# The last supertile of a 1x1 depthwise-separable convolution, worked off tile by tile

## The chip, the core and the metric

The kernel runs on one core of one Trainium2 chip. A core has a matrix engine (TensorE, PE in the profile, with its weight loads listed as PEld), a vector engine (VectorE, DVE), a scalar engine (ScalarE, ACT), GpSimd (POOL), and SyncE (SP), which here issues the transfers; sixteen DMA engines move data between the device memory and the on-chip buffer. TensorE writes its sums to a separate accumulator memory (the `ps` tiles)[...]. The metric is the device time of one execution in microseconds (us), lower is better; the profile's span is a little shorter than that time because it runs from the first to the last instruction.

## What is computed

```python
x:  (1, 384, 384, 384) bf16     # batch, height, width, channels
dw: (1, 1, 384) bf16            # depthwise weights, one tap (k = 1)
pw: (384, 384) bf16             # pointwise weights

out = x * dw[0, 0]              # k = 1: no neighbours, no padding
return einsum("bhwc,cd->bhwd", out, pw)
```

With one tap the depthwise part is a scaling of the channels, so the whole is one matrix product: 147,456 rows of 384 channels times a 384 x 384 matrix whose row c is `dw[c] * pw[c]`. Each of x and the output is 113 MB.

## The kernel before

The 147,456 rows are worked off in 288 *supertiles* of 512 rows. A supertile passes four stations: its x lies in the on-chip buffer with rows on the partitions; DVE transposes it in 32 x 32 blocks of 32-bit words (two channels in a word), so that channels lie on the partitions; TensorE multiplies; ACT copies the four accumulators to an output buffer as bf16; SyncE stores. Transfers are grouped by ten supertiles (`LMAX`), in three rotating x buffers and three rotating output buffers; the first and the last groups are cut smaller.

```python
def _groups(n_super):
    head, tail = [[1, 1, 2, 2, 4]], [[6, 4], [4, 2, 1, 1]]   # the last two supertiles are chunks of their own
    ...
LONG, LONG_AT = 2, [8, 148]     # the last two supertiles' x is loaded at supertiles 8 and 148
```

The block transposes leave each 32-row group of partitions with another set of x rows. Group q of partitions holds a 32-word slice of channels of the rows of accumulator q, so one supertile is four independent products of 32 partitions each, run at the same time on four row groups of the array. The weights `w_r` are laid out so that every group of 32 partitions holds the same channel pairs:

```python
steps = [(b, par) for b in range(4) for par in range(2)] + [(4, 0), (5, 0), (4, 1), (5, 1)]

def supertile(s, rv):
    for b, par in steps:                     # 6 channel blocks x 2 channels of a word: 12 groups
        for q in range(4):                   # 4 matmuls of 32 rows, at the same time
            if q == 0 and par == 0 and b in (0, 3):
                nc.tensor.wait_ge(s_t[s][b // 3], rv)
            ...
            mm = nc.tensor.matmul(
                PS[s][:, q, :D],
                lhsT=Ts[s][32 * q : 32 * q + 32, b, par::2],
                rhs=w_r[32 * q : 32 * q + 32, b, par, :],
                start=(b, par) == steps[0], stop=(b, par) == steps[-1],
                tile_position=(32 * q, 0))
            if (b, par) == steps[0] and q == 0:
                mm._wait_ge(s_a[s], rv)      # the accumulators were copied out
            if (b, par) in ((2, 1), (5, 1)) and q == 3:
                mm.then_inc(s_pe)            # half done, all done
...
with nc.tensor.Fori(0, NS // 2, 1) as it:    # all 288 supertiles, two per turn of the loop
    rv = nc.tensor.to_reg(it + 1)
    for s in range(2):
        supertile(s, rv)
```

All four accumulators of a supertile end in its last group. The copies out, by ACT alone except for the very last supertile:

```python
for jj, (t, j) in enumerate(order):
    s = jj % 2
    ...
    if jj + 1 == NS:                         # last supertile: two copies on ACT, two on DVE
        nc.vector.wait_ge(s_pe, 2 * jj + 2)
        ...
        nc.scalar.wait_ge(s_pe, 2 * jj + 2)
        for q in (0, 2):
            nc.scalar.copy(Ov[:, q, j, :], PS[s][:, q, :D]).then_inc(s_a[s])
            nc.vector.tensor_copy(Ov[:, q + 1, j, :], PS[s][:, q + 1, :D]).then_inc(s_d)
        continue
    a = nc.scalar.copy(Ov[:, :, j, :], PS[s][:, :, :D])
    a._wait_ge(s_pe, 2 * jj + 2)
    a.then_inc(s_a[s])
    ...
    if jj + 2 < NS:
        transposes(*order[jj + 2])           # DVE runs two supertiles ahead
```

The last supertile is stored in two parts of 192 KB, each once one ACT and one DVE copy are done; the one before it in one part of 384 KB.

Of the kernel before, what the change touches and what calls it, by code (L numbers as in the profile page):

```python
# [7 lines left out]
BF16 = mybir.dt.bfloat16  # L8
F32 = mybir.dt.float32
U32 = mybir.dt.uint32  # L10
# [3 lines left out]
NR = 3  # L14
LONG = 2
LONG_AT = [8, 148]
# [11 lines left out]
def kernel(  # L28
# [12 lines left out]
    nc = tc.nc  # L41
    P = nc.NUM_PARTITIONS
    B, H, W, C = x.shape
    assert dw.shape[0] == 1 and dw.shape[1] == 1, "only k=1 depthwise supported"
    D = pw.shape[1]
# [7 lines left out]
    NS = N // 512  # L53
# [8 lines left out]
    n_parts = [2 if c[0] + 1 == len(groups) and (c[4] > 1 or c[3] + 1 == NS) else 1 for c in chunks]  # L62
# [6 lines left out]
    pw_n = consts.tile([P, 3, D], BF16, name="pw_n")  # L69
    eye = consts.tile([P, P], BF16, name="eye")  # L70
    sel = consts.tile([P, 2, 32], F32, name="sel")
    sel_w = consts.tile([P, 3, 2, 4, 32], BF16, name="sel_w")
# [8 lines left out]
    Xl = bufp.tile([P, 4 * LONG, C], BF16, name="Xl")  # L81
# [5 lines left out]
    s_xl = [nc.alloc_semaphore(f"s_xl{n}") for n in range(LONG)]  # L87
# [15 lines left out]
    with tc.tile_critical(sync_engine=mybir.EngineType.Pool, no_gpsimd_drain=True):  # L103
        def x_of(t):
            g, i, off, first, L = chunks[t]
            n = first + LONG - NS
            if n >= 0:
                return Xl[:, 4 * n : 4 * n + 4, :], s_xl[n], 16
            n = sum(len(ls) > i for ls in groups[g % NR : g + 1 : NR])
            return Xs[g % NR][:, 4 * off : 4 * (off + L), :], s_x[g % NR][i], 16 * n  # L110

        def load_x(t, eng=nc.sync):
            g, i, off, first, L = chunks[t]
            dst, sem, _ = x_of(t)
            rows = xf[512 * first : 512 * (first + L), :]
            if first + LONG < NS:
                src = rows.rearrange("(p s) c -> p (s c)", p=P)
                dst = dst.rearrange("p s c -> p (s c)")
                if i == 0 and g >= NR:
                    je = g_end[g - NR]  # L120
                    eng.wait_ge(s_t[je % 2][1], je // 2 + 1)
            else:
                src = rows.rearrange("(a k q) c -> q a k c", k=4, q=4)
            eng.dma_start(dst, src).then_inc(sem, 16)

        def store(t, k):
            g, i, off, first, L = chunks[t]
            je = first + L * (k + 1) // n_parts[t] - 1
            src = Os[g % NR][:, 4 * off * D : 4 * (off + L) * D]
            rows = of[512 * first : 512 * (first + L), :]  # L130
            if first + LONG < NS:
                dst = rows.rearrange("(q p j) d -> p q (j d)", q=4, p=P)
                src = src.rearrange("p (q e) -> p q e", q=4)
                e = L * D // n_parts[t]
                dst, src = dst[:, :, e * k : e * k + e], src[:, :, e * k : e * k + e]
            else:
                dst = rows.rearrange("(m q) d -> m (q d)", q=4)
            if first + 1 == NS:
                je = first
                part = slice(2 * D * k, 2 * D * k + 2 * D)  # L140
                nc.sync.wait_ge(s_d, k + 1)
                nc.sync.wait_ge(s_a[je % 2], je // 2 + 2 + k)
                nc.sync.dma_start(dst[:, part], src[:, part]).then_inc(s_o[g % NR], 16)
                return
            nc.sync.wait_ge(s_a[je % 2], je // 2 + 2)
            nc.sync.dma_start(dst, src).then_inc(s_o[g % NR], 16)


# [5 lines left out]
        todo = []  # L154
        for t, (g, i, off, first, L) in enumerate(chunks):
            if 0 < t < NT - LONG:
                todo.append((g_end[g - NR] if g >= NR else -1, load_x, (t,)))
            for k in range(n_parts[t]):
                todo.append((first + L * (k + 1) // n_parts[t] + 1, store, (t, k)))
        for _, f, a in sorted(todo, key=lambda a: a[0]):  # L160
            if f is load_x and chunks[a[0]][4] == LMAX and chunks[a[0]][0] == 1:
                nc.sync.wait_ge(x_of(1)[1], 16)
            if f is store and a[0] == 0:

                for _ in range(28):
                    nc.sync.wait_ge(s_pw, 16)
            f(*a)
# [8 lines left out]
        w_eng = [1, 0, 1, 1, 1, 1]  # L176
# [77 lines left out]
        with nc.tensor.Fori(0, NS // 2, 1) as it:  # L254
            rv = nc.tensor.to_reg(it + 1)
            for s in range(2):
                supertile(s, rv)

# [13 lines left out]
        def transposes(t, j):  # L272
            g, i, off, first, L = chunks[t]
            jj = first + j
            s = jj % 2
            X, sem, n = x_of(t)
# [41 lines left out]
        for jj, (t, j) in enumerate(order):  # L318
# [5 lines left out]
            if jj + 1 == NS:  # L324
                nc.vector.wait_ge(s_pe, 2 * jj + 2)
                nc.vector.wait_ge(s_o[g % NR], 16 * sum(map(len, groups[g % NR : g : NR])))
                nc.scalar.wait_ge(s_pe, 2 * jj + 2)
                for q in (0, 2):
                    nc.scalar.copy(Ov[:, q, j, :], PS[s][:, q, :D]).then_inc(s_a[s])  # L329
                    nc.vector.tensor_copy(Ov[:, q + 1, j, :], PS[s][:, q + 1, :D]).then_inc(s_d)  # L330
                continue
# [4 lines left out]
            if jj in LONG_AT:  # L336
                load_x(NT - LONG + LONG_AT.index(jj), nc.scalar)
# [32 lines left out]
```

## Time and profile before

| | |
|---|---|
| time, median of 3 runs | 574.69 us (574.32 to 576.32) |
| span of the profiled execution | 573.0 us |
| granted TensorE clock | 1.00 of full speed |
| DVE busy | 507.5 us (89%) |
| ACT busy | 418.7 us (73%) |
| moved | 226.88 MB, mean 396 GB/s |

The span holds three stretches. In the first 7 us the weights are loaded and scaled and the first x arrives. The longest by far is the run of 288 supertiles. What follows the last matmul is the tail: copies, the last store, and the closing of the program. Busy time is the sum of an engine's instructions; the *chain that ended last* is found by walking back from the last instruction to what released it, and tells which engine set the end. Matmuls overlap in the array, so four matmuls of 0.32 us each that start together count once in busy time. Engines named with a q are their instruction queues.

### The profile page before, as it was taken

Reading aid. Unit: us, or ns where it says so; the run is one execution under the profiler, and the core shown is the slowest. Engines: PE = TensorE matmul, PEld = TensorE weight load, DVE = VectorE, ACT = ScalarE, POOL = GpSimd, SP = SyncE. Lnnn points to the kernel's source line nnn. Section 1 sums busy time; section 2 is a strip of 40 time slices with the busy share of each in tenths; the row PEclk is TensorE's granted clock in tenths of the full one; section 3 lists DMA queues with packets and bytes.
Section 4 is the critical chain, followed back from the end, with each engine's and each line's share of the span. In section 5 each row is a group of like instructions: output and inputs, shape, how many; then the busy total and the mean of one; then the engine's idle time right before and its main releaser. Section 6 shows DMA issues by size and latency. Waiting matters only on the chain.

```text
span 573.0 us, 29705 instructions
## 1 busy us (share of the span) xinstructions
PE 566.9 (99%) x13867; PEld 420.6 (73%) x13867; DVE 507.5 (89%) x584; ACT 418.7 (73%) x297; POOL 0.5 (0%) x5
## 2 busy tenths in 40 slices
PE   8999999999999999999999999999999999999997
PEld 4777777777777777777777777777777777777775
DVE  7888898898898899889889889889988988988985
ACT  6777777777777777777777777777777777777775
POOL 0000000000000000000000000000000000000000
PEclk9999999999999999999999999999999999999999
DMA  8999999999999999999999999999999999999677
GB/s 332 434 357 430 420 423 433 436 425 421 428 416 413 391 394 434 390 394 399 428 390 396 404 418 395 420 395 427 409 380 427 400 387 391 427 399 380 259 289 248
DMA packets 26468, 226.88 MB, mean 396 GB/s; under 512 B 1241, under 2 KB 7002, under 8 KB 22618
## 3 DMA queue, kind: packets, MB, share of 16 engines
q1 hardware_dynamic: 25424, 226.01, 97.4%
q10 hardware_dynamic: 1034, 0.79, 0.4%
q14 instruction: 9, 0.07, 0.0%
q8 instruction: 1, 0.02, 0.0%
HBM read 113.54 MB, written 113.25 MB: 396 GB/s over the span
## 4 chain that ended last, share of the span: by engine, by line
PE 97%; DMA 1%; ACT 0%; DVE 0%; SPq 0%; issue 0%; DVEq 0%; POOLq 0%
PE ps L195 97%; DMA X<-in_x_dram 1%; DMA out_dram<-O 0%; ACT O L332 0%; DVE T L282 0%; DVE O L330 0%; DVEq L103 0%; SPq L151 0%; SPq L150 0%; SPq L365 0%; POOLq L103 0%; POOLq L354 0%
## 5 line engine op out<-in xcount | busy, mean ns | idle before, releaser
L195 PE MATMUL ps<-w_r,T 32*128 32x384 bf16 x13824 | 561.8, 321 | 0.7 <-DVE T L282 0.7
L282 DVE STREAM_TRANSPOSE T<-X 128x384 uint32<-128x384 uint32 x572 | 500.7, 878 | 56.1 <-DMA X<-in_x_dram 1.7
L195 PEld LDWEIGHTS ps<-w_r,T 32*128 32x128 bf16 x13824 | 419.0, 93 | 143.8 <-issue 1.4
L332 ACT CAST O<-ps 128x1536 bf16<-128x1536 f32 x287 | 412.7, 1438 | 148.1 <-PE ps L195 148.1
L295 ACT CAST w_r<-ps 128x768 bf16<-128x768 f32 x5 | 3.6, 820 | 0.8 <-PE ps L245 0.8
L282 DVE STREAM_TRANSPOSE T<-Xl 128x384 uint32<-128x384 uint32 x4 | 3.5, 878 | 0.4
L330 DVE CAST O<-ps 128x384 bf16<-128x384 f32 x2 | 1.0, 552 | 3.0 <-DMA out_dram<-O 3.0
L212 PE MATMUL ps<-const-bfloat16-1.0 32*128 32x384 bf16 x24 | 2.2, 515 | 1.1 <-PEq L354 1.1
L245 PE MATMUL ps<-pw_n,sel_w 64*128 64x384 bf16 x16 | 2.9, 514 | 0.1
L245 PEld LDWEIGHTS ps<-pw_n,sel_w 64*128 64x128 bf16 x16 | 0.8, 114 | 2.2 <-DMA pw_n<-in_pw_dram 1.2
L270 ACT ACT_TABLE_LOAD x1 | 1.3, 1283 | 1.5 <-POOLq L103 1.5
L212 PEld LDWEIGHTS ps<-const-bfloat16-1.0 32*128 32x128 bf16 x24 | 0.7, 117 | 1.4 <-issue 1.4
L300 DVE TENSOR_REDUCE sel<-eye 128x64 f32<-128x128 bf16 x1 | 0.3, 286 | 1.5 <-POOL eye L260 1.5
L295 DVE CAST w_r<-ps 128x768 bf16<-128x768 f32 x1 | 1.0, 958 | 0.5 <-PE ps L245 0.5
L329 ACT CAST O<-ps 128x384 bf16<-128x384 f32 x2 | 0.9, 482 | 0.5 <-PE ps L195 0.5
L307 DVE COPY dw_f<-ps 128x3 f32<-128x3 f32 x1 | 0.2, 161 | 0.9 <-PE ps L225 0.9
L310 DVE TENSOR_SCALAR sel_w<-sel,dw_f 128x256 bf16<-128x256 f32 x3 | 0.9, 350 | 0.0
L225 PEld LDWEIGHTS ps<-const-bfloat16-1.0,dw_row 1*128 1x128 bf16 x3 | 0.3, 115 | 0.4 <-DMA dw_row<-in_dw_dram 0.4
L270 ACT COPY warm<-const-float32-0.0 128x1 f32<-128x1 f32 x2 | 0.3, 190 | 0.0
L260 POOL TENSOR_SCALAR_AFFINE_SELECT eye<-const-bfloat16-1.0 128x128 bf16<-128x128 bf16 x1 | 0.3, 293 | 0.6 <-POOLq L103 0.6
L225 PE MATMUL ps<-const-bfloat16-1.0,dw_row 1*128 1x1 bf16 x3 | 0.3, 176 | 0.0
L354 POOL MEMSET const-uint8-127<- 128x1 uint8 x1 | 0.1, 102 | 0.0
(3 smaller groups left out, 0.3 us busy)
## 6 DMA issues: line engine op xcount, KB each, us to landing
X<-in_x_dram SPq DMA_DIRECT2D x26, 3840.0 KB, 21.3
out_dram<-O SPq DMA_DIRECT2D x26, 3840.0 KB, 27.2
X<-in_x_dram SPq DMA_DIRECT2D x3, 1536.0 KB, 17.7
out_dram<-O SPq DMA_DIRECT2D x4, 768.0 KB, 9.9
out_dram<-O SPq DMA_DIRECT2D x2, 1536.0 KB, 15.1
X<-in_x_dram SPq DMA_DIRECT2D x3, 768.0 KB, 7.5
X<-in_x_dram SPq DMA_DIRECT2D x1, 2304.0 KB, 19.3
out_dram<-O SPq DMA_DIRECT2D x1, 2304.0 KB, 11.1
```

The costliest lines, as they stand in the source:

```text
L195: mm = nc.tensor.matmul(PS[s][:, q, :D], lhsT=Ts[s][32 * q : 32 * q + 32, b, par::2], rhs=w_r[32 * q : 32 * q + 32, b, par, :], start=(b, ...
L212: nc.tensor.matmul(PS[0][:, 2 * (i % 2) + i // 2, :D], lhsT=ones[32 * i : 32 * i + 32, 0:P], rhs=ones[32 * i : 32 * i + 32, :], start=True ...
L225: mm = nc.tensor.matmul(PS[1][:, 0, D + k : D + k + 1], lhsT=dw_row[:, P * k : P * k + P], rhs=ones[0:1, 0:1], start=True, stop=True,)
L245: mm = nc.tensor.matmul(PS[(k + 1) % 2][:, 2 * r + v, :D], lhsT=sel_w[64 * v : 64 * v + 64, k, r, :, :].rearrange("p q w -> p (q w)"), rhs ...
L260: nc.gpsimd.affine_select(out=eye[:], in_=ones[:, 0:P], pattern=[[-1, P]], compare_op=mybir.AluOpType.is_equal, fill=0.0, base=0, channel_ ...
L270: nc.scalar.copy(warm[:, s : s + 1], nc.const_aps.tensor(0.0, [P, 1], F32)).then_inc(s_a[s])
L282: ins = nc.vector.transpose(out=Tw[:, 3 * h : 3 * h + 3], in_=Xw[:, :, j, 96 * h : 96 * h + 96].rearrange("p k (b w) -> p b k w", w=32),)
L295: o = nc.vector.tensor_copy(out, in_) if e == 0 else nc.scalar.copy(out, in_)
L310: nc.vector.tensor_scalar_mul(sel_w[:, k], sel[:].unsqueeze(2).to_broadcast([P, 2, 4, 32]), dw_f[:, k : k + 1]).then_inc(s_sw)
L329: nc.scalar.copy(Ov[:, q, j, :], PS[s][:, q, :D]).then_inc(s_a[s])
L330: nc.vector.tensor_copy(Ov[:, q + 1, j, :], PS[s][:, q + 1, :D]).then_inc(s_d)
L332: a = nc.scalar.copy(Ov[:, :, j, :], PS[s][:, :, :D])
```

## The change

The last two supertiles are treated differently; the first 286 are not touched.

1. **Matmuls of the last supertile.** Its x is loaded by channel block, so that after the transposes all 128 partitions (or 64 of them) hold different channels of the same rows. One accumulator then needs two matmuls of 128 rows (four blocks of 32 words, two channels in a word) and two of 64 rows (the remaining two blocks), in place of twelve of 32 rows. The accumulators are finished one after the other and each signals for itself, so that the copies can start while TensorE works on the next.
2. **x of the last supertile** comes in eight loads (four of 16 and four of 8 pieces for each of 32 partitions, 128 bytes a piece), one every 20 supertiles from supertile 40 on, where it was one load at supertile 148.
3. **A second weight tile `w_k`** with the channel blocks on different partitions is copied together from `w_r` by eight small transfers inside the on-chip buffer, at supertile 40, into the space of `pw` and the selection matrix, which are no longer used by then.
4. **The copies.** The supertile before the last is copied half by ACT and half by DVE; the last one's four accumulators alternate ACT, DVE, ACT, DVE in the order in which they are finished (0, 2, 1, 3).
5. **The stores.** The supertile before the last leaves in two parts of 192 KB, the last one in three: accumulators 0 and 2 (192 KB), then 1 (96 KB), then 3 (96 KB). Rows of the last supertile now lie one per partition and accumulator, so its packets are 768 bytes where they were 1536.
6. **The loop** runs one turn less; supertile 286 and the new matmuls stand after it.

The diff, cut to what the above speaks of:

```diff
-LONG = 2
-LONG_AT = [8, 148]
+LONG_AT = 8
+LAST_AT = range(40, 200, 20)
+PARTS = [slice(0, 4, 2), slice(1, 2), slice(3, 4)]
...
-    pw_n = consts.tile([P, 3, D], BF16, name="pw_n")
+    raw = consts.tile([P, 3 * (D + 256)], BF16, name="raw")
+    pw_n = raw[:, 0 : 3 * D].rearrange("p (k d) -> p k d", d=D)
+    sel_w = raw[:, 3 * D :].rearrange("p (k r q w) -> p k r q w", r=2, q=4, w=32)
+    w_k = raw[:, 0 : 4 * D].rearrange("p (k r d) -> p k r d", r=2, d=D)
...
-    Xl = bufp.tile([P, 4 * LONG, C], BF16, name="Xl")
+    Xl = bufp.tile([P, 4, C], BF16, name="Xl")
+    Xk = bufp.tile([P, 24, 64], BF16, name="Xk")
...
+        def load_last(n):
+            rows = xf[512 * (NS - 1) :, :].rearrange("(m i) c -> i m c", i=32)
+            if n < 4:
+                dst = Xk[32 * n : 32 * n + 32, 0:16, :]
+                src = rows[:, :, 64 * n : 64 * n + 64]
+            else:
+                h, e = (n - 4) // 2, n % 2
+                dst = Xk[32 * n - 128 : 32 * n - 96, 16:24, :]
+                src = rows[:, 8 * h : 8 * h + 8, 256 + 64 * e : 320 + 64 * e]
+            nc.sync.dma_start(dst, src).then_inc(s_xk, 16)
+
+        def fill_w_k():
+            for sem, v in w_all:
+                nc.sync.wait_ge(sem, v)
+            for q in range(4):
+                rows = slice(32 * q, 32 * q + 32)
+                for k, b in enumerate((q, 4 + q % 2)):
+                    nc.sync.dma_start(w_k[rows, k], w_r[rows, b]).then_inc(s_wk, 16)
...  (in store: supertile 286 in two parts, the last one in three)
+            elif first + 2 == NS:
+                dst = rows.rearrange("(m q) d -> m (q d)", q=4)
+                part = slice(2 * D * k, 2 * D * k + 2 * D)
+                dst, src = dst[:, part], src[:, part]
+                nc.sync.wait_ge(*((s_a[0], NS // 2 + 1) if k == 0 else (s_d, 1)))
             else:
-                dst = rows.rearrange("(m q) d -> m (q d)", q=4)
...
+                dst = rows.rearrange("(m p) d -> p m d", p=P)[:, PARTS[k], :]
+                src = src.rearrange("p (m d) -> p m d", d=D)[:, PARTS[k], :]
+                if k < 2:
+                    nc.sync.wait_ge(s_a[1], NS // 2 + 1 + k)
+                if k != 1:
+                    nc.sync.wait_ge(s_d, (2, 0, 3)[k])
...
+        todo += [(at, load_last, (n,)) for n, at in enumerate(LAST_AT)]
+        todo.append((LAST_AT[0], fill_w_k, ()))
...
-        with nc.tensor.Fori(0, NS // 2, 1) as it:
+        with nc.tensor.Fori(0, NS // 2 - 1, 1) as it:
             rv = nc.tensor.to_reg(it + 1)
             for s in range(2):
                 supertile(s, rv)
+        supertile(0, NS // 2)
+
+        Tk = Ts[1][:].rearrange("p b (i r) -> p (b i) r", r=2)
+
+        def last_mm(m, at, k, par, rows, start, stop):
+            return nc.tensor.matmul(
+                PS[1][:, m, :D],
+                lhsT=Tk[rows, at : at + P, par],
+                rhs=w_k[rows, k, par, :],
+                start=start,
+                stop=stop,
+                tile_position=(rows.start, 0),
+            )
+
+        nc.tensor.wait_ge(s_wk, 128)
+        nc.tensor.wait_ge(s_a[1], NS // 2)
+        for v in range(2):
+            nc.tensor.wait_ge(s_t[1][v], NS // 2)
+            for par in range(2):
+                for h in range(2):
+                    last_mm(v + 2 * h, 384 * v + 256, 1, par, slice(64 * h, 64 * h + 64), par == 0, False)
+            for h in range(2):
+                for par in range(2):
+                    mm = last_mm(v + 2 * h, 384 * v + 128 * h, 0, par, slice(0, P), False, par == 1)
+                mm.then_inc(s_pe)
...  (in transposes: the last supertile's two, from Xk, same size as the others)
...
-            if jj + 1 == NS:
+            if jj + 2 == NS:
                 nc.vector.wait_ge(s_pe, 2 * jj + 2)
                 nc.vector.wait_ge(s_o[g % NR], 16 * sum(map(len, groups[g % NR : g : NR])))
-                nc.scalar.wait_ge(s_pe, 2 * jj + 2)
-                for q in (0, 2):
-                    nc.scalar.copy(Ov[:, q, j, :], PS[s][:, q, :D]).then_inc(s_a[s])
-                    nc.vector.tensor_copy(Ov[:, q + 1, j, :], PS[s][:, q + 1, :D]).then_inc(s_d)
+                a = nc.scalar.copy(Ov[:, 0:2, j, :], PS[s][:, 0:2, :D])
+                a._wait_ge(s_pe, 2 * jj + 2)
+                a.then_inc(s_a[s])
+                nc.vector.tensor_copy(Ov[:, 2:4, j, :], PS[s][:, 2:4, :D]).then_inc(s_d)
+                continue
+            if jj + 1 == NS:
+                for n, m in enumerate((0, 2, 1, 3)):
+                    o = (nc.vector.tensor_copy if n % 2 else nc.scalar.copy)(Ov[:, m, j, :], PS[s][:, m, :D])
+                    o._wait_ge(s_pe, 2 * jj + 1 + n)
+                    o.then_inc(s_d if n % 2 else s_a[s])
                 continue
```

## What was predicted

> **What bounds the kernel now.** I read the page first, then its chain, then the last 12 us as a timeline, then the transfers of that stretch. From the page, the engines' busy time and the chain by engine and line:
>
> ```profile
> PE 566.9 (99%) x13867; PEld 420.6 (73%) x13867; DVE 507.5 (89%) x584; ACT 418.7 (73%) x297; POOL 0.5 (0%) x5
> ...
> PE 97%; DMA 1%; ACT 0%; DVE 0%; SPq 0%; issue 0%; DVEq 0%; POOLq 0%
> ...
> L195 PE MATMUL ps<-w_r,T 32*128 32x384 bf16 x13824 | 561.8, 321 | 0.7 <-DVE T L282 0.7
> ```
>
> The reader is to see that TensorE waits 0.7 us in all behind its 13,824 main matmuls. It runs without a gap from 7.05 us to 568.8 us, so only what happens before 7.05 and after 568.8 can be won without fewer matmuls. The change leaves the first part alone and works on the second. The timeline from 566 us (start, length, engine, line, what):
>
> ```profile
> 565.72 3.11 PE L195 MATMUL ps<-w_r,T 32*128 32x384 bf16 x72
> 565.91 2.53 PEld L195 LDWEIGHTS ps<-w_r,T 32*128 32x128 bf16 x61
> 566.44 2.29 SPq L146 DMA_DIRECT2D out_dram<-O  x2
> 566.93 1.44 ACT L332 CAST O<-ps 128x1536 bf16<-128x1536 f32 x1 [0.51 <-PE ps L195]
> 568.88 0.86 ACT L329 CAST O<-ps 128x384 bf16<-128x384 f32 x2 [0.51 <-PE ps L195]
> 568.88 1.02 DVE L330 CAST O<-ps 128x384 bf16<-128x384 f32 x2 [3.02 <-DMA out_dram<-O]
> 569.46 0.84 SPq L143 DMA_DIRECT2D out_dram<-O  x2
> ```
>
> Here the two evacuations of consecutive supertiles start 568.88 - 566.93 = 1.95 us apart: that is the matmul time of one supertile, 12 groups of four concurrent 32-row matmuls, 1.95 / 12 = 0.1625 us a group. After the last matmul, both engines make two copies each, one after the other (1.02 us on DVE); the second pair of copies ends at 569.90, and the last store is issued at 569.93. The transfers of the last 13 us (size, issue to landing in us):
>
> ```profile
> out_dram<-O SPq DMA_DIRECT2D x3, 384.0 KB, 2.6
> out_dram<-O SPq DMA_DIRECT2D x1, 768.0 KB, 4.1
> out_dram<-O SPq DMA_DIRECT2D x2, 192.0 KB, 2.0
> ```
>
> So the last 192 KB land 2.0 us after 569.93, at 571.93, and the 573.0 us span has 1.09 us of closing semaphores left, which the change does not touch. The tail behind the last matmul group is thus: 0.37 us until the copies start, 1.02 us of copies, 0.03 us, 2.0 us of store, 1.09 us of closing.
>
> [...] The kernel before never changes mode between its main matmuls[...]. The trace has 93 ns for 32 rows and 114 for 64 rows in the cold start-up; no 128-row load is in it. [...] The main loop spans two supertiles and the periods in the trace are even (1946 to 1951 ns over all 288)[...]; the trace's shortest data packets are 768 B.
>
> **The change part by part.**
>
> (1) Matmul time of the last supertile. 48 matmuls of 32 rows (12 groups x 0.1625 = 1.95 us) become 8 matmuls of 64 rows, two at a time on the two halves of the array (4 x 0.1625), and 8 of 128 rows, one at a time (8 x 0.1625): again 12 x 0.1625 = 1.95 us. Nothing won or lost, except four mode changes (32 to 64, 64 to 128, 128 to 64, 64 to 128). One matmul lasts 322 ns in the trace and the next group starts 162 ns after it, so at most some 160 ns of pipeline depth can be exposed per change. I take half, 0.08 us: 4 x 0.08 = 0.32 us lost on the path. This term is the softest of the sum.
>
> (2) Tiles finish one by one. Where all four accumulators ended in the last group before, they now end in groups 4, 6, 10 and 12 (tiles 0, 2, 1, 3). With the first group of the last supertile starting at 568.51 - 11 x 0.1625 = 566.72 and 0.37 us from a group's start to a copy's start, tile 0 is ready at about 567.6 + two changes, tile 2 at 567.9 + two, tile 1 at 568.55 + four, tile 3 at 568.88 + four. Three of the four copies now lie beside matmuls; on the path stays one copy on DVE, about 0.55 us (L330's mean), ending at 568.88 + 0.55 + 0.32 = 569.75, against 569.90 before. Without the mode changes this step wins 0.47 us, with them 0.15.
>
> (3) The supertile before it is emptied by ACT and DVE, half each. A 128x768 copy takes 0.82 us on ACT and 0.96 on DVE (both are in the start-up, line 295), against 1.44 for the whole on ACT. From 566.93 they end at 567.75 and 567.89. This is what makes (2) possible: with the old 1.44 us, ACT would be busy to 568.37 and tile 0 would wait. Its own effect on the end is nil, beyond the 384 KB store leaving 0.5 us earlier, in two parts.
>
> (4) The last store is a third as wide: tile 3 alone, 96 KB in 768-byte packets, in place of 192 KB. Issue to landing was 2.6 us for 384 KB and 2.0 for 192, so 0.3 us per 96 KB: about 1.7 us. Won: 0.3 us. SyncE needs 0.34 to 0.38 us per issue and has five now: about 567.8, 568.15, 568.55, then 569.4 and 569.8; the last two are 0.4 apart, so SyncE is just free for the last one.
>
> (5) x for the last supertile comes in eight loads with 128-byte packets: 4 x 512 + 4 x 256 = 3072 packets, one load every 20 supertiles (39 us), in place of one load of 512 packets. By the trace's packet records a 768-byte packet holds an engine for 36 ns and a 1536-byte packet for 65, so about 7 ns plus 0.038 ns per byte: 12 ns for 128 bytes. 3072 x 12 / 16 = 2.3 us over 300 us. The main loads land some 18 us before their first transpose, and stores some 13 us before their buffer is written again, so this is hidden even if a small packet costs three times as much.
>
> (6) The eight copies that build the second weight tile, and the waits ahead of them, cost SyncE 8 x 0.35 = 3 us once, at supertile 40; hidden by the same 13 us. The transposes of the last supertile keep their size (384 words, 0.88 us each) and their place.
>
> Sum: -0.47 (copies) + 0.32 (mode changes) - 0.3 (last store) = -0.45 us of 574.69, 0.08%: 574.2.
>
> **The rivals.** (a) The mode changes cost their whole 160 ns each, and the 128-row weight loads are not hidden behind the matmul before them, for each uses the whole array, while today's loads go to another row group than the running matmul[...]. Together some +1.0 against -0.77: 574.9 or 575.0. The page speaks neither for nor against: weight loads are 73% busy but overlapped fourfold. [...] (c) The tail of the store is hidden anyway: if the landing is latency and not bytes, (4) is worth 0.1, and the time is 574.4. (d) The 128-byte loads delay the bulk stream, which is busy without a break (a DMA share of 1.01 from 10 to 400 us by the windows): if a small packet took as long as a 512-byte one it would still be only 3072 x 26 / 16 = 5 us over 300, within the slack of 13 to 18 us. No change of the time.
>
> **Range and chances.** The sum without mode cost is -0.77 and with rival (a) +0.2 to +0.3; the three runs of the kernel before reach from 574.32 to 576.32, which is wider than the effect. I predict 574.2 us, with 573.5 to 575.3 for 8 in 10[...]. 2% would be 11.5 us; the whole tail after the last matmul is 4.5 us, so faster by over 2% is out of reach: 0.5%. Slower by over 2% needs a broken overlap in the bulk, which nothing in the profile suggests: 1%. Within 2%: 98.5%.
>
> **What would show each step.** In the changed kernel's timeline the 48 matmuls of supertile 287 and the 16 new ones should span 3.9 us plus the mode cost: a start-to-start distance over 0.1625 us at the four changes alone confirms (1), over it at every 128-row matmul confirms (a)[...]. Three of the four single-tile copies should start before the last matmul does, and one 0.55 us DVE copy should stand after it. The last store should land in about 1.7 us. The idle time of the transposes for x should stay at 1.7 us; if it grows, (d) is right and my step (5) wrong. I would be wrong outright if TensorE gained idle time anywhere before 560 us.

## The result and the profile after

| | kernel before | changed kernel |
|---|---|---|
| time, median (range) | 574.67 us (574.32 to 576.32), 4 runs | 579.69 us (578.56 to 580.62), 4 runs |
| span of the profiled execution | 573.0 us | 578.9 us |
| ratio after / before, 95% interval | | 1.0081 [1.0053, 1.0109] |

The change costs 5.0 us where 0.45 were to be won. The page of the changed kernel does not show it at first sight (engines, the chain by engine, then the two groups of main and new matmuls with busy time, mean ns, and idle time before them):

```profile
PE 566.6 (98%) x13835; PEld 413.7 (71%) x13835; DVE 509.1 (88%) x585; ACT 418.6 (72%) x297; POOL 0.5 (0%) x5
...
PE 97%; DMA 1%; DVE 0%; SPq 0%; issue 0%; DVEq 0%; POOLq 0%
...
L225 PE MATMUL ps<-w_r,T 32*128 32x384 bf16 x13776 | 559.8, 321 | 1.3 <-DVE T L346 1.3
...
L293 PE MATMUL ps<-raw,T 64*128 64x384 bf16 (+1 forms) x16 | 2.5, 329 | 0.0
```

TensorE is busy as long as before (566.6 against 566.9 us) and the chain still runs through it. The 1.3 us before its first main matmul lie ahead of 8 us; by stretches, TensorE is busy for 192.00 of the 192 us from 8 to 200 us, for 200.00 of the 200 from 200 to 400 and for 160.00 of the 160 from 400 to 560, in both kernels. So nothing was lost before 560 us, and the end has to be read. The timeline of the changed kernel from 566.5 us (start, length, engine, line, what, idle time before it and its releaser):

```profile
566.44 6.22 SPq L173 DMA_DIRECT2D out_dram<-O  x6
...
566.81 2.45 PE L293 MATMUL ps<-raw,T 64*128 64x384 bf16 x16
566.92 0.80 ACT L391 CAST O<-ps 128x768 bf16<-128x768 f32 x1 [0.51 <-PE ps L225]
566.93 0.96 DVE L394 CAST O<-ps 128x768 bf16<-128x768 f32 x1 [1.37 <-PE ps L225]
...
567.78 0.48 ACT L398 CAST O<-ps 128x384 bf16<-128x384 f32 x1
...
568.11 0.56 DVE L398 CAST O<-ps 128x384 bf16<-128x384 f32 x1 [0.22 <-PE ps L293]
...
568.97 0.48 ACT L398 CAST O<-ps 128x384 bf16<-128x384 f32 x1 [0.71 <-PE ps L293]
569.30 0.56 DVE L398 CAST O<-ps 128x384 bf16<-128x384 f32 x1 [0.63 <-PE ps L293]
```

The compute part is what the change wanted: copies lie beside the matmuls, and the last one, on DVE, ends at 569.86 us. After it the span still has 9 us. The first line has a hint: six issues on SyncE fill 6.22 us. Singly, the one at 566.44 took 2.21 us and one at 568.70 took 1.93, where the median of all stores of that line is 0.39 (ns, shortest/median/longest; the longest is an issue at 16.5 us):

```profile
L173 SPq DMA_DIRECT2D out_dram<-O x42: 372/389/12683, 10.8 to 572.2; - x42
```

What happens after 569.86 stands in the transfers of the changed kernel from 560 to 578.9 us (the first two rows are 40 equal slices of 0.47 us; then size and median us from issue to landing):

```profile
DMA  9997000799999950000599149999600000000000
GB/s 374 377 371 273 29 20 20 267 361 384 364 315 343 320 176 26 26 20 26 174 336 322 49 169 367 345 324 303 202 24 23 23 26 23 24 23 21 0 0 0
...
out_dram<-O SPq DMA_DIRECT2D x2, 384.0 KB, 5.9
out_dram<-O SPq DMA_DIRECT2D x3, 192.0 KB, 2.5
out_dram<-O SPq DMA_DIRECT2D x2, 96.0 KB, 3.9
```

From slice 29 to slice 36, 573.7 to 577.5 us, the transfers run at 21 to 26 GB/s. Some 370 GB/s are 16 engines' work, so 23 is one engine's: fifteen of the sixteen have nothing left, and one still works off its part of the last stores. The same stretch by engine (length, then busy us of PE, PEld, DVE, ACT, POOL, the granted clock, the mean DMA share, GB/s):

```profile
568.00:574.00 6.00, 1.26 (x9) 0.42 (x8) 1.12 (x2) 0.74 (x2) 0.00 (x0) 1.00 0.63 209
574.00:578.90 4.90, 0.00 (x0) 0.00 (x0) 0.00 (x0) 0.00 (x0) 0.00 (x0) 0.54 0.05 17
```

No compute engine does anything in the last 4.9 us; the DMA share of 0.05 is about one engine of sixteen. The mean share hides this: 0.05 looks like idle. Now the same row of the kernel before, from 560 to 573.1 us (40 slices of 0.33 us):

```profile
GB/s 380 371 380 366 380 150 23 23 23 19 169 366 371 375 371 347 338 338 326 321 293 33 159 328 324 328 64 0 338 385 403 239 371 371 291 5 0 0 0 0
```

The lone engine was there already: "23 23 23 19" at 562 to 563.3 us, and once more for a moment at slice 21. It drained its backlog just ahead of the end; the zeros at slice 27 (568.8 us) are the first moment at which nothing at all was under way.

The size of the backlog can be read from one transfer, the last store of 3840 KB, issued at about 535 us. The transfers from 530 us on, in the kernel before and in the changed one:

```profile
out_dram<-O SPq DMA_DIRECT2D x1, 3840.0 KB, 16.5
```

```profile
out_dram<-O SPq DMA_DIRECT2D x1, 3840.0 KB, 24.2
```

The trace also has the moment at which each of the 16 engines reported its part as landed: fifteen of them had finished this store after 10.8 us, in both kernels. So the sixteenth was 16.5 - 10.8 = 5.7 us late before, and 24.2 - 10.8 = 13.4 after.

Taking the differences between that engine's landings in the kernel before, a large store keeps it busy for 10.46 us (327 ns for each of its 32 packets; the median over all engines' packets of that size is 291 ns, 9.3 us), and a large load for 9.10 (median from 330 to 480 us). That is 19.56 us for each ten supertiles, whose matmuls take 19.5. **This engine alone has no spare time while loads and stores both run**: in the kernel before, the landing of its large stores creeps from 25.9 us (store of about 106 us) to 29.0 (496 us). It catches up only at the end. The last x load is issued at 511.7 us; from then on stores alone are left, 10.46 us of work in 19.5, and the landing falls from 29.0 to 16.5 us, in the changed kernel from 36.8 to 24.2. What is not worked off by then is waited for.

### The profile page after: what moved, and what is told of

It reads as the page before. It is cut to its first block, busy times and chain, and to the rows that moved or that the text cites. A ratio compares the mean times of both kernels' runs of the same rounds, so it can differ in the third digit from the quotient of the medians.

```text
span 578.9 us, 29656 instructions
## 1 busy us (share of the span) xinstructions
PE 566.6 (98%) x13835; PEld 413.7 (71%) x13835; DVE 509.1 (88%) x585; ACT 418.6 (72%) x297; POOL 0.5 (0%) x5
## 4 chain that ended last, share of the span: by engine, by line
PE 97%; DMA 1%; DVE 0%; SPq 0%; issue 0%; POOLq 0%
PE ps L225 97%; DMA X<-in_x_dram 1%; PE ps L293 0%; DVE T L346 0%; DVE O L398 0%; SPq L180 0%; SPq L179 0%; SPq L435 0%; POOLq L109 0%; POOLq L424 0%
## 5 line engine op out<-in xcount | busy, mean ns | idle before, releaser
L225 PEld LDWEIGHTS ps<-w_r,T 32*128 32x128 bf16 x13776 | 411.4, 93 | 149.7 <-issue 1.7
L293 PE MATMUL ps<-raw,T 64*128 64x384 bf16 (+1 forms) x16 | 2.5, 329 | 0.0
L275 PE MATMUL ps<-raw 64*128 64x384 bf16 x16 | 2.2, 399 | 0.3 <-ACT w_r L359 0.2
L346 DVE STREAM_TRANSPOSE T<-Xl 128x384 uint32<-128x384 uint32 x2 | 1.8, 878 | 0.2
L336 DVE STREAM_TRANSPOSE T<-Xk 128x384 uint32<-128x384 uint32 x2 | 1.2, 580 | 0.5 <-PE ps L225 0.4
```

The costliest lines, as they stand in the source:

```text
L225: mm = nc.tensor.matmul(PS[s][:, q, :D], lhsT=Ts[s][32 * q : 32 * q + 32, b, par::2], rhs=w_r[32 * q : 32 * q + 32, b, par, :], start=(b, ...
L275: mm = nc.tensor.matmul(PS[(k + 1) % 2][:, 2 * r + v, :D], lhsT=sel_w[64 * v : 64 * v + 64, k, r, :, :].rearrange("p q w -> p (q w)"), rhs ...
L293: return nc.tensor.matmul(PS[1][:, m, :D], lhsT=Tk[rows, at : at + P, par], rhs=w_k[rows, k, par, :], start=start, stop=stop, tile_positio ...
L336: ins = nc.vector.transpose(out=Tw[:, v], in_=Xw[:, v])
L346: ins = nc.vector.transpose(out=Tw[:, 3 * h : 3 * h + 3], in_=Xw[:, :, j, 96 * h : 96 * h + 96].rearrange("p k (b w) -> p b k w", w=32),)
```

## The experiments

The theory (T): the transfers that the change adds in mid-run (eight loads of 128-byte pieces, eight weight copies) put the lagging engine further back, and it reaches the end too late. The first rival (R1): the new tail is itself the cause, by more and smaller stores that crowd SyncE and the engines at the end. A second (R2), once the transfers were suspected: transfers as a whole are short, not one engine. A third (R3): the lag differs from execution to execution by itself. (In the expectations below T is theory A, R1 theory B and R3 theory C.) R3 falls at once: the changed kernel's shortest time, 578.56 us, is above the longest of the kernel before beside it, 576.32.

The table has all runs. "Landing" is issue to landing of the 3840 KB store of about 535 us; its first fifteen engines took 10.8 us in all of them but e8 and e16, where they took 11.3. Landing and span are those of the one profiled execution, which need not be the median: the changed kernel's took 580.62 us, e7's 578.95. One execution each of e5 and e6 was in a slower state of the chip (601.55 and 593.43 us) and is left out.

| run | median us | ratio to before [95%] | landing, us | span, us |
|---|---|---|---|---|
| kernel before | 574.4 to 574.7 by session | | 16.5 | 573.0 |
| changed kernel | 579.69 | 1.0081 [1.0053, 1.0109] | 24.2 | 578.9 |
| e1: old tail, new transfers | 578.95 | 1.0066 [1.0040, 1.0092] | 22.2 | 577.2 |
| e2: new tail, last x in one load | 574.62 | 1.0001 [0.9991, 1.0011] | 18.4 | 573.0 |
| e3: new tail, no weight copies | 574.46 | 0.9995 [0.9986, 1.0004] | 17.6 | 572.8 |
| e4: new tail, neither | 573.98 | 0.9992 [0.9985, 0.9999] | 17.1 | 572.0 |
| e5: a load split 120 + 8 | 585.82 | 1.0189 [1.0162, 1.0216] | 27.3 | 584.1 |
| e6: a load split 112 + 16 | 583.03 (583.00, 583.03, 588.94) | 1.0192 [1.0127, 1.0257] | 27.1 | 581.2 |
| e7: before, 4 needless loads | 576.32 | 1.0028 [1.0014, 1.0042] | 22.9 | 577.2 |
| e8: before, 8 needless loads | 582.58 | 1.0126 [1.0102, 1.0150] | 27.4 | 581.3 |
| e9: weight copies by GpSimd | 574.45 | 1.0004 [0.9993, 1.0014] | 17.4 | 572.5 |
| e10: e9, other shape of loads | 574.53 | 0.9996 [0.9983, 1.0008] | 17.8 | 572.8 |
| e11: before, 8 loads on 14 engines | 579.54 | 1.0087 [1.0069, 1.0104] | 23.0 | 577.5 |
| e12: before, 8 half loads on 16 engines | 580.34 | 1.0100 [1.0083, 1.0117] | 22.1 | 577.9 |
| e13: changed, one large load left out | 574.17 | 0.9994 [0.9985, 1.0004] | 15.0 | 572.5 |
| e14: e9, one large load left out | 574.27 | 0.9994 [0.9979, 1.0009] | 13.5 | 572.9 |
| e15: before, 8 loads on 4 engines | 575.06 | 1.0004 [0.9995, 1.0013] | 16.8 | 574.0 |
| e16: before, 8 loads on 8 engines | 586.55 | 1.0215 [1.0173, 1.0258] | 27.2 | 582.9 |

### Which part of the change costs the time: e1 to e4

**e1** is the kernel before, tail and all, with the change's transfers put in: the eight loads bring the last x into the old buffer's second half, and the eight weight copies fill a tile that nobody reads. The last supertile's product is therefore not the reference's.

```diff
-LONG_AT = [8, 148]
+LONG_AT = [8]
+LAST_AT = range(40, 200, 20)
...  (load_last and fill_w_k as in the change)
+        todo += [(at, load_last, (n,)) for n, at in enumerate(LAST_AT)]
+        todo.append((LAST_AT[0], fill_w_k, ()))
```

> The kernel before with its own matmuls, copies and stores, but with the change's transfers: x of the last supertile in eight loads of 128-byte pieces and the eight weight copies (the last supertile's x lies in another order than its transposes suppose, so its 512 output rows are other numbers; every instruction keeps its size). Theory A (extra transfer work falls on one DMA engine that already lags the others and has no slack, so the last store waits for it): 578 to 581 us, and in the trace the 16th engine's landings fall about 20 us behind the others by 549 us. Theory B (the tail's own five small stores and their issue make the 5 us): 574.7 us, like the kernel before. Theory C (the lag differs from run to run by itself): anything, with a spread of several us between rounds.

It took 578.95 us, 4.5 more than the kernel before: the transfers alone make the loss, with the old tail, its two-engine copies and its last stores untouched. R1 falls. The tail of its transfers, 560 to 584 us (slices of 0.6 us), has the lone engine in the same place:

```profile
GB/s 387 374 366 64 23 33 364 371 358 346 329 198 179 330 174 84 404 364 374 126 23 23 23 26 26 26 5 0 0 0 0 0 0 0 0 0 0 0 0 0
```

**e2** is the changed kernel, with the last x brought by one load from ScalarE's queue at supertile 148, as before. It lies in the buffer in the old order, so the last supertile is not the reference's; every instruction is kept.

```diff
-        todo += [(at, load_last, (n,)) for n, at in enumerate(LAST_AT)]
-                nc.vector.wait_ge(s_xk, 128)
+                nc.vector.wait_ge(s_xk, 16)
+            if jj == LASTX_AT:      # 148
+                nc.scalar.dma_start(Xk..., xf[512 * (NS - 1) :, :].rearrange("(a k q) c -> q a k c", k=4, q=4)).then_inc(s_xk, 16)
```

> The changed kernel with the last supertile's x in one load of 512 packets of 768 bytes, as the kernel before loads it (order of the rows not what the transposes suppose, so 512 output rows are other numbers), weight copies kept. Theory A: the eight loads are most of the extra work (192 packets per engine against 16 for the copies), so 574.5 to 576.5 us. Theory B: 579.7 us.

**e3** keeps the eight loads and leaves out the eight weight copies (the last supertile's weights are then old content).

```diff
-        todo.append((LAST_AT[0], fill_w_k, ()))
-        nc.tensor.wait_ge(s_wk, 128)
```

> The changed kernel with the eight 128-byte loads, but without the eight weight copies and the wait for them (the last supertile multiplies with what lies in that space). Theory A: the copies are 16 packets of 1536 bytes per engine, about 1 us of one engine's time, so 1 us is won: 578 to 579.5 us. Theory B: 579.7 us.

**e4** makes both edits: the new tail and nothing of the new transfers.

> The changed kernel with both taken away: one load for the last x as before, no weight copies; matmuls, copies and stores of the new tail all stay. Theory A: the lagging engine has the kernel before's work again, and the tail shows what it is worth: 574.0 to 574.6 us, a little below the kernel before. Theory B: 579.7 us.

Measured: 574.62, 574.46 and 573.98 us. Taking away either kind of transfer gets nearly the whole loss back. For e3 that was not expected (578 to 579.5): the two costs do not add. Against e4 the loads alone (e3) cost 0.48 us, the copies alone (e2) 0.64, both together (the changed kernel) 5.7.

The landings say where the sum breaks. Stores issued at about 204 us and at about 496 us, in the kernel before and then in the changed one:

```profile
out_dram<-O SPq DMA_DIRECT2D x1, 3840.0 KB, 26.6
out_dram<-O SPq DMA_DIRECT2D x1, 3840.0 KB, 29.0
```

```profile
out_dram<-O SPq DMA_DIRECT2D x1, 3840.0 KB, 30.2
out_dram<-O SPq DMA_DIRECT2D x1, 3840.0 KB, 36.8
```

At 204 us the landings of e4, e3, e2 and the changed kernel are 27.5, 28.2, 29.1 and 30.2 us: +0.7 for the four small loads made so far, +1.6 for the copies, +2.7 for both. Up to here it nearly adds up. At 496 us they are 29.7, 30.2, 31.0 and 36.8: +0.5, +1.3, and +7.1 for both. Between 330 and 480 us the lagging engine took 9.57 us for a large load in the changed kernel (mean of eight), against 9.09 to 9.10 in e2, e3 and e4 and 9.16 in the kernel before. In e1, e7 and e8 too, which came to lag about as far, its loads took 9.32, 9.43 and 9.61. Being far behind is not the whole reason: in e13 and e14 below, just after this engine had been relieved of 9 us, its next three loads took 9.9 to 10.9 us. What slows its loads was not found out, nor why two delays come out as more than their sum.

The time for which the eight copies held SyncE does not matter: it made one store start at 89.9 us in place of 86.7, but the lagging engine had earlier work until 105 us.

What is left of the backlog at the end costs time only above a threshold. With the new tail it lies near a landing of 17 us: at 13.5 (e14), 15.0 (e13) and 17.1 (e4) the last of all landings is at 571.8, 571.4 and 570.9 us, so less backlog brings nothing, and from 17.1 on it moves to 571.9 at 18.4 (e2) and 577.8 at 24.2 (changed), 6.9 us for 7.1. So e4, which has no added transfers, is the measurement of the tail that was predicted: its last 96 KB land in

```profile
out_dram<-O SPq DMA_DIRECT2D x2, 96.0 KB, 1.7
```

1.7 us, the span is 1.0 us shorter, and the time is 573.98 against 574.41 in the same session: 0.43 us won, by the interval 0.1 to 0.9.

### Giving the engine more or less to do: e7, e8, e13, e14

If it is a matter of the transfers' amount and not of their form, plain needless loads must do the same to the kernel before. **e7** and **e8** add four and eight loads of 288 KB (2304 bytes for each of 128 partitions) to it, each into the space of `pw`, from supertile 40 on, one every 20 supertiles. By the trace each takes every engine about 0.74 us (8 packets with a median of 93 ns).

```diff
+            nc.sync.dma_start(pw_n[:].rearrange("p k d -> p (k d)"),
+                xf[0:384, :].rearrange("(p s) c -> p (s c)", p=P)).then_inc(s_dose, 16)
```

> The kernel before, plus four needless loads of 288 KB into the weights' idle space, one every 20 supertiles from 40 on. Each gives every DMA engine 8 packets of 2304 bytes, about 0.75 us: 3 us on the lagging engine, spread evenly. Theory A: the kernel before has some 1 to 1.5 us left before the lagging engine shows, so 575.5 to 577.5 us. If only the copies and the 128-byte pieces hurt through something of their own: 574.4 us.

> The same with eight such loads, 6 us of work on every engine. Theory A: 3 us more than with four at least, 578.5 to 582 us; above the threshold each microsecond of transfer work on the lagging engine is a microsecond of time. Otherwise 574.4 us.

Measured: 576.32 us for four (+1.8; 574.88 to 578.95) and 582.58 for eight (+8.0). The doses are 4 x 0.74 = 3.0 and 5.9 us of each engine's time. In the median the first is partly hidden; the second comes out larger than it went in, where one for one was expected above the threshold. The landing of the last large store grew from 16.5 to 22.9 (in the longest of e7's executions) and 27.4. The threshold and the growth of the first four runs are both in these two.

**e13** takes work away: the changed kernel without the large x load of the twentieth group (its ten supertiles compute on old x, so a twenty-ninth of the output is not the reference's, and TensorE's work is the same). **e14** does the same to e9.

```diff
+SKIP = [20]
-            eng.dma_start(dst, src).then_inc(sem, 16)
+            if g not in SKIP:
+                eng.dma_start(dst, src).then_inc(sem, 16)
```

> The changed kernel with one of its large x loads left out (group 20, 3.84 MB of 113; the supertiles of that group work on what lies in the buffer, so 5120 output rows are other numbers; nothing else is changed). No engine of the core ever waits for that load in the traces. Theory A: the lagging DMA engine gets 9.1 us back, the last store is no longer late, 573.8 to 574.4 us. Theory B or C: 579.7 us.

> The same left out of the kernel whose weight copies are made by GpSimd. Theory A: that kernel sits just at the threshold, so relief shows what the new tail is worth once no DMA engine is late: 573.8 to 574.1 us, 0.4 us under the kernel before. If the 574.45 us of that kernel are not due to the lag: 574.4 us.

Measured: 574.17 and 574.27 us. With 9 us of transfer taken off each engine, all of the changed kernel's added transfers cost nothing: 5.5 us came back. e14 lies between its two expectations, and its interval (0.9979 to 1.0009) does not tell them apart. The loads and copies still delay the engine, but from a smaller backlog. e13's tail from 560 to 584 us (slices of 0.6 us):

```profile
GB/s 371 374 210 15 0 225 381 371 321 330 320 47 328 312 364 330 318 231 54 0 0 0 0 0 0 0 0 0 0 0 0 0 0 0 0 0 0 0 0 0
```

The lone engine is hardly there: at 562 us, where it worked for 1.3 us in the kernel before, the row falls to 15 and then to 0, so all sixteen are done. A landing of 15.0 or 13.5 us brings no more than one of 17.1 (e4), as a threshold has it.

### One engine or all of them: e5, e6, e11, e12, e15, e16

R2, that bandwidth as a whole is short, is not excluded by doses on all engines. **e5** was to take one engine's share away: the load of group 20 is cut into 120 and 8 partitions; **e6** is its control, with the cut at 112.

```diff
+            if g in SPLIT:      # [20]; CUT = 120 (e5), 112 (e6)
+                eng.dma_start(dst[:CUT], src[:CUT]).then_inc(sem, 16)
+                eng.dma_start(dst[CUT:], src[CUT:]).then_inc(sem, 16)
+                return
```

> The changed kernel, complete, with one of its 30 large x loads (group 20, issued at about 355 us) split by partitions into 120 and 8[...]. Theory A, if the engine left out is the lagging one: it catches up by one load, 9.1 us, its last store no longer comes late, and the time is that of the new tail without extra transfers, 573.9 to 574.4 us. If the lagging engine is another: 579.5 us or more[...]. Theory B or C: 579.7 us, unchanged.

> Control for the split: the same load cut into 112 and 16 partitions[...]. The splitting is there, the relief is not. Theory A: 579 to 580.5 us, as the changed kernel. If the split itself (two smaller transfers, another order) were what helps: below 576 us.

Both failed as a test: 585.82 and 583.03 us, longer than the changed kernel. From 360 to 380 us, where the load runs, in e5 and then in the changed kernel (columns as above; the last two are DMA share and GB/s):

```profile
360.00:380.00 20.00, 20.00 (x503) 14.76 (x495) 18.08 (x21) 14.77 (x11) 0.00 (x0) 1.00 0.97 235
```

```profile
360.00:380.00 20.00, 20.00 (x500) 14.69 (x493) 17.99 (x22) 14.67 (x11) 0.00 (x0) 1.00 1.00 401
```

At a mean DMA share of 0.97 against 1.00 the engines move 235 GB/s in place of 401: cut like this, the load is far dearer in their time (e6: 0.98 and 268). And e5 relieved the wrong engine: of the 23 landings of its two parts (15 and 8, so the larger part left one engine out) the last two stand alone, 6.5 us after the others and 1.2 us apart, so the lagging engine worked on both parts. It is one of the eight that took the 8-partition part.

**e11** and **e12** were to give the dose of e8 to seven or to eight engines only, by an outer dimension of that size on both sides.

```diff
-                xf[0:384, :].rearrange("(p s) c -> p (s c)", p=P)
+                xf[0:24 * u, :].rearrange("(u v s) c -> u v (s c)", u=7, v=8)      # e12: u=8
```

> The kernel before with eight needless loads of 8 packets of 2304 bytes per engine as in the eight-fold dose[...] (outer dimension seven, 56 partitions). Theory A says that only work on the lagging engine counts.[...] If it is the eighth: 574.3 to 575 us. If it is the fifth to seventh: 580 to 583 us. If the sum of transfer work counts (7/16 of the full dose): 576 to 578 us.

> The same[...] (outer dimension eight, 64 partitions). Theory A:[...] 580 to 583 us, like the dose on all sixteen, with half of its bytes. If the sum of transfer work counts: 577 to 579 us.

They did not test that. In the trace the semaphore of such a load moves 15 times in e11 and 16 times in e12, where with u and v in the other order (e15 and e16 below) it moves 5 and 9 times. In e11 the first move comes 0.6 to 0.9 us after the issue, the next 11 us later or more. The two x loads on ScalarE's queue in the kernel before show the same: five moves each, the first 1.1 and 1.0 us after the issue, the other four after 18 and 68 us. So an early move is read here as no landing, and 15 moves as 14 engines. That u and v were merged when the kernel was built, as they follow each other in memory, is the author's inference; the traces show the counts alone. A load of e11 has 56 packets and one of e12 has 64, four for each of 14 and of 16 engines: half doses, by an estimate of 0.37 us per load and engine (four packets of 93 ns). They cost 5.1 and 5.9 us, more than the four full loads of e7, whose total for an engine is the same (8 x 0.37 = 3.0 us). They are twice as many and go on to supertile 180; which of the two makes the difference was not tried.

**e15** and **e16** repeat it with u and v in the other order.

```diff
-                xf[0:384, :].rearrange("(p s) c -> p (s c)", p=P)
+                xf[0:24 * u, :].rearrange("(v u s) c -> u v (s c)", u=4, v=8)      # e16: u=8
```

> The kernel before with eight needless loads, 8 packets of 2304 bytes (about 0.73 us) each per engine as in the eight-fold dose, but with an outer dimension of four that cannot be folded away[...]. Theory A with the lagging engine not among these four: 574.3 to 575 us. If any transfer work anywhere counts: 576 us or more, and if the lagging engine is among the four: 581 to 583 us.

> The same with an outer dimension of eight[...]. Theory A with the lagging engine the fifth to eighth: 580 to 583 us, like the dose on all sixteen. If it is one of the upper eight: 574.3 to 575 us.

Here the semaphore moves 5 and 9 times, and 4 and 8 of the moves are landings (below): four and eight engines, each with the same 18 KB per load as in e8. The four cost little, if anything (575.06 us, 1.0004 [0.9995, 1.0013]), the eight cost 12.1 us. By the times alone it could still be the amount, which in e15 is half of that in e16. The landings settle it. The four parts of the needless load of 200.7 us land in e15 between 16.5 and 18.4 us; of the eight parts of that of 199.4 us in e16, seven land by 19.3 us and one at 24.8. And the large store of about 204 us lands after 26.4 us in e15, as in the kernel before (26.6), but after 31.2 us in e16. So R2 falls: the same work for each engine is next to free on the four of e15 (+0.6 us), where no part lands late, and dear on the eight of e16 (+12.1), where one lands 5.5 us after the seven others. The lagging engine took part in e16 and not in e15. The traces count the engines of a transfer and do not number them; the engine numbers in the expectations are the author's assumption, and which one it is was not shown. Eight engines cost more than all sixteen (586.55 against 582.58): up to 204 us each load set the lagging engine back by (31.2 - 26.6) / 4 = 1.2 us in e16, but by (30.0 - 26.6) / 4 = 0.9 in e8. Why is not explained. The tails of e15 and of e16 from 560 to 584 us (slices of 0.6 us):

```profile
GB/s 358 369 371 371 225 20 23 225 371 374 339 328 324 63 325 307 4 389 320 364 238 0 0 0 0 0 0 0 0 0 0 0 0 0 0 0 0 0 0 0
```

```profile
GB/s 410 310 394 381 369 90 23 31 23 23 325 371 340 358 333 251 20 26 26 26 26 31 268 333 86 266 389 361 312 23 23 23 26 26 26 15 0 0 0 0
```

In e15 the lone engine shows for two slices and is done; in e16 it stands at 20 to 31 GB/s three times, and the last time is the end of the kernel.

### A whole kernel without the cost: e9, e10

**e9** computes the reference: the change with the eight weight copies made by GpSimd, which is idle, and not by transfers. **e10** also gives the small loads an outer dimension of four.

```diff
-                    nc.sync.dma_start(w_k[rows, k], w_r[rows, b]).then_inc(s_wk, 16)
+                    nc.gpsimd.tensor_copy(w_k[rows, k], w_r[rows, b]).then_inc(s_wk)
...  (e10)
-            rows = xf[512 * (NS - 1) :, :].rearrange("(m i) c -> i m c", i=32)
+            rows = xf[512 * (NS - 1) :, :].rearrange("(m u v) c -> u v m c", u=4, v=8)
```

> The changed kernel, complete, but the second weight tile is copied by GpSimd (idle until then; each copy stays on its partitions) in place of eight transfers. The 128-byte loads stay. Theory A: as the run without weight copies, 574.2 to 574.7 us, level with the kernel before. If the copies cost only through SyncE's issue order: the same, so this run separates nothing there. If GpSimd's copies hold up DVE's transposes, a gap of some us appears on TensorE near 45 to 60 us and the time is 576 or more.

> The run above, and the eight 128-byte loads written with an outer dimension of four[...]. Theory A: as the run with neither, 573.8 to 574.2 us, faster than the kernel before by 0.4 us, and a complete kernel. If the number of small packets counts and not whose they are: 574.5 us or more.

Measured: 574.45 us, 1.0004 [0.9993, 1.0014]. The copies' row in e9 (count, then ns shortest/median/longest, and first and last start):

```profile
L148 POOL COPY raw<-w_r x8: 812/819/826, 80.6 to 86.3; 32x768 bf16<-32x768 bf16 x8
```

Eight copies of 0.82 us on an idle engine in place of eight transfers are worth 5.2 us (579.69 to 574.45). But e9 is level with the kernel before and not ahead of it: the loads cost about what the tail wins (0.48 us by e3 and e4). In e10 the outer dimension left a load on all engines (16 landings per load), so it is a second measurement of e9. No version that computes the whole and beats the kernel before was found.

## Why the prediction was right or wrong

It was 574.2 us (573.5 to 575.3); measured 579.69. **The step that failed is the overlap in (5) and (6): that the added transfers are "hidden by the same 13 us".** In its place the runs showed one DMA engine without spare time in mid-run. It finishes the last large store 13.4 us behind the others (5.7 before), and the stores after it wait for its older work; without the added transfers the time is 573.98 us (e4). By its own steps:

- **(1) Matmul time, right, a little short.** Starts lie 162 to 163 ns apart within a mode, 253 to 258 ns apart at the four changes, and 170 to 175 once after each: about 0.1 us a change where 0.08 was put. The last matmul starts at 568.93 against 568.51 us, 0.42 later where 0.32 was put. Rival (a) is wrong: 128-row matmuls start 162 to 175 ns apart, while each of their weight loads takes 98 to 101 ns, so the loads are hidden. (Its +1.0 was the author's estimate: 4 x 0.16 = 0.64 us for the changes, and the rest for weight loads of 128 rows, which the kernel before does not have.) There is no gap at the loop's end: from 560 to 566.5 us the matmul groups start 162 to 163 ns apart throughout.
- **(2) and (3) Copies, right.** The last DVE copy runs from 569.30 to 569.86 us; its predicted end was 569.75. The halves took 0.80 and 0.96 us. Of the other three copies two start before the last matmul does and the third 0.04 us after it.
- **(4) Last store, right** once nothing else is in its way: 1.7 us in e4, and 2.2 for 192 KB there. Rival (c), that the landing is latency, fits less well. In the changed kernel the last 96 KB are issued at 572.22 us, 2.4 late after the long issues on SyncE, and land 5.6 us later, since one engine has older work.
- **The sum of these, right within a wide margin.** e4 is this part: -0.43 us against -0.45, but with an interval of -0.1 to -0.9.
- **(5) and (6) Added transfers, wrong.** The costs were fair: the 128-byte packets took 13 ns in the records (12 assumed). The slack that (5) counts on is how early a transfer lands before its consumer in mid-run. It was there, and held even with landings of 36.8 us: TensorE was busy for all of the 552 us from 8 to 560. But slack towards a consumer is not idle time of the engine. The lagging engine, with 19.56 us of work in each 19.5, had none in mid-run. It did not hide the added work but put it off until the last store, and there the consumer is the end of the kernel. An estimated 4.5 us of its time (192 small packets of 13 ns, 2.5 us, and 2.0 us for the copies, the landing of the store of about 106 us in e2 against e4, 28.9 - 26.9) came out as a landing later by 24.2 - 17.1 = 7.1 us. Not in proportion: the small loads alone made 0.5 of it, the copies alone 1.3.
- **Rival (d), "no change of the time", wrong for the same reason.** It took the mean DMA share (1.01) as the state of all engines, and divided the packets by 16. Its test, more idle time of the transposes, looked in the wrong place: that stayed (1.5 us for x).
- **"TensorE gains idle time before 560 us"** as the one sign of being wrong outright did not appear; the kernel got slower after its last matmul.

It could have been read beforehand, in the profile of the kernel before: the row of GB/s at 23 from 562 us, and 16.5 us for a store that fifteen engines finish in 10.8.

Open: why the lagging engine needs 327 ns per store packet, which of the sixteen it is, and what slows its loads in mid-run, so that two delays come out as more than their sum.

## What to carry to other kernels

Where a kernel's transfers run without a break, as here (a mean DMA share of 1.01 from 10 to 400 us), read the slowest DMA engine and not the mean. A tail at a sixteenth of the full rate (23 of 370 GB/s), or a last large store whose last part lands long after the others (16.5 us against 10.8), was the sign of a backlog here, and added transfers lengthened it (24.2 us). Count added transfer work for that engine against what it has left by the end of the run, not against how early its data land. The eight copies inside the buffer were better made by an idle compute engine than by transfers: 574.45 us in e9 against 579.69.

## What the runs showed of the hardware

- One DMA engine of sixteen was slower on the same work (327 ns a store packet against a median of 291 in the kernel before). A second one did not stand out: in the last large store the fifteen others land within 0.2 us. Neither its number nor the reason is in the traces.
- In the changed kernel a store's issue on SyncE took 0.39 us in the median, and two took 2.2 and 1.9 us near the end, when one engine was far behind. Whether the backlog holds the issue up was not tested: one at 16.5 us, where no engine stands out, took 12.7.
- With one large load cut at partition 120 or 112, the rate from 360 to 380 us was 235 and 268 GB/s in place of 401.
- A change of array mode cost about 0.1 us with 384 columns: 253 to 258 ns to the next start in place of 162, and some 10 ns more at the one after.
- The transposes of the last supertile took 0.58 us for 384 words per partition, where those of the others, and step (6) of the prediction, had 0.88.
